# Feed-forward block borders of a fused attention and two-FFN kernel: earlier split of x, and low parts on GpSimd

## The chip, the cores and the metric

One core of one Trainium2 chip runs the whole program. The metric is the device time in microseconds of one execution; several executions were timed, and one more was profiled.

## The reference, cut to what matters

```python
x = attention(q_l, k_l, v_l, q_g, k_g, v_g)          # 4 batches x 544 tokens, 512 features (windowed + global)
xn = x / sqrt(mean(x * x) + 1e-6) * rms_g            # first FFN
g, val = xn @ w_gate, xn @ w_val                     # 512 -> 1536
y = (g * sigmoid(g) * val) @ w_out                   # 1536 -> 512
h = y @ w_in                                         # second FFN, 512 -> 2048
out = (P(h) / Q(h)) @ w_out2                         # a rational function, 2048 -> 512
```

The weights arrive as 64-bit floats and are turned into pairs of 32-bit parts on the chip.

## The kernel before, in words

Three stages follow each other: attention (with part of the first FFN between its steps), the rest of the first FFN, the second FFN. TensorE multiplies float32 data in a reduced form, so every operand is split into a high part (rounded by ScalarE) and a low part (the difference), and each product is three matmuls: high times high, weight low times high, weight high times low.

**First FFN** (class FFN1). The 2176 tokens are cut into 8 blocks (blk) of 288 or 256 tokens, the 1536 hidden features into 3 groups (grp) of 4 tiles k. A *task* is one group of one block; there are 24, all blocks of group 0 first. The generator `units` (L646) gives a task as 12 units:
- `up` (L599): for one k, the products of xt (the split x, four chunks c) with w_gate and w_val into two PSUM banks psg and psv. Two units, chunks 0 and 1, then 2 and 3; 12 matmuls each, at L606 (high x), L607 (weight low) and L608 (low x), chunk by chunk.
- `act` (L610): ScalarE reads psg (L617, or L619 in group 0), VectorE multiplies with psv (L621, and L620 in group 0), ScalarE makes ah (L622), and the low part al (L624) is made by VectorE, or by GpSimd in group 0.
- `down` (L628): 12 matmuls (L633 to L635) of the *previous* task's ah and al with w_out into psA, one of four m a unit; then y is written or added (L639, L641). In a task the four come as one behind the first k and three behind the second.
- `split` (L585): ScalarE writes the high part of the four xt chunks (L595), VectorE the low part (L596), GpSimd in group 0. It is called once a task, behind the last `up`, for the next task. Each xt chunk has one buffer, so its split waits until the last matmul that reads the old chunk is done.

A task is 144 matmuls. **Weights** (class Weights): a conversion takes one tile of 512 columns through ScalarE (L83, L85), VectorE (L91, L92, L95), GpSimd (L99), ScalarE for the high part (L104) and `lo_eng` for the low part (L105). Two scratch tiles cv go round. `step` runs the stages of up to two conversions; in the loop at L884 it is called once a unit from n = 72 on, with VectorE as `lo_eng` (L904). In attention and in the second FFN `lo_eng` is GpSimd.

The order on each engine is not the order of the code: a scheduler places the instructions by priority (the order of the code, unless `high_priority` moves a block ahead by some places) and by its own estimate of durations. Every engine then runs its list strictly in that order, and waits where a row's inputs or buffers are not there. In attention the list `target` (L843 to L846) says how many units are to be placed by each step.

## Time and profile before

| | |
|---|---|
| median of 3 runs | 1089.58 us (1089.46 to 1092.65) |
| profiled execution | 1092.84 us, span 1091.1 us |
| TensorE (PE) busy | 1007.9 us, 92% |
| weight loads (PEld) busy | 907.3 us, 83% |
| VectorE (DVE) busy | 792.8 us, 73% |
| ScalarE (ACT) busy | 600.2 us, 55% |
| GpSimd (POOL) busy | 373.4 us, 34% |

Busy is the share of the span in which an engine has an instruction under way, including time in which that instruction itself is held up. The sum over the span hides the stages: attention ends at about 321 us, the first FFN at about 692 us. The x behind a number counts instructions; in the first FFN the number of matmuls in a stretch says better than the busy share how fast TensorE went.

### The profile page before, as it was taken

The numbers are of one execution on the slowest core, as the hardware profiler recorded it, in microseconds if no ns is written. First come the engines' busy times: TensorE is split into PE (matmuls) and PEld (weight loads), VectorE is DVE, ScalarE is ACT, GpSimd is POOL, SyncE is SP. The second block draws the span as 40 slices with busy tenths as digits, with TensorE's granted clock in tenths as the row PEclk, the third lists the DMA queues.
The fourth block names the chain that finished last, engine by engine and source line by source line (L and its number), as shares of the span: only waits on it lengthen the run. The fifth ranks groups of instructions, "written<-read, shape, count | busy, mean of one in ns | idle before, by whom it ended". The sixth has DMA issues, their size and how long they took to land.

```text
span 1091.1 us, 23781 instructions
## 1 busy us (share of the span) xinstructions
PE 1007.9 (92%) x9368; PEld 907.3 (83%) x9368; DVE 792.8 (73%) x1750; ACT 600.2 (55%) x1347; POOL 373.4 (34%) x421
## 2 busy tenths in 40 slices
PE   3669898998989989999999999999999999999997
PEld 2547777877778889899989999888989989898895
DVE  4674554655529999873797453599898998989987
ACT  3644545645447675552654342466666666666675
POOL 5461212212135743220231111354343543435433
PEclk7669999999999999999999999999999999999999
DMA  7943544434116330650430113500000000000000
GB/s 161 276 127 84 114 123 98 108 100 105 32 39 253 117 116 20 212 174 2 155 117 8 33 40 87 185 1 1 30 1 20 11 1 30 1 30 1 1 31 20
DMA packets 104432, 83.46 MB, mean 76 GB/s; under 512 B 63744, under 2 KB 91392, under 8 KB 104320
## 3 DMA queue, kind: packets, MB, share of 16 engines
q1 hardware_dynamic: 102592, 75.64, 23.8%
q0 software_dynamic: 1728, 6.29, 1.8%
q8 instruction: 74, 1.21, 0.5%
q14 instruction: 38, 0.31, 0.1%
HBM read 62.64 MB, written 10.75 MB: 67 GB/s over the span
## 4 chain that ended last, share of the span: by engine, by line
PE 50%; DVE 29%; ACT 8%; DMA 4%; issue 4%; POOL 3%; SPq 2%; ACTq 0%; POOLq 0%; DVEq 0%
PE psg L606 3%; PE psg L608 3%; DVE q L725 3%; PE psS L349 3%; PE psv L608 3%; DVE q L713 3%; PE psv L607 3%; PE psH L703 3%; PE psH L704 3%; PE psv L606 3%; PE psg L607 3%; PE psH L705 3%; PE psB L738 3%; PE psA L633 3%; PE psB L739 3%
## 5 line engine op out<-in xcount | busy, mean ns | idle before, releaser
L130 POOL TENSOR_SCALAR gh<-p 128x384 fp32r<-128x384 f32 (+1 forms) x96 | 58.1, 605 | 210.2 <-DVE p L727 185.8
L703 PE MATMUL psH<-yt,w_h 128*128 128x384 f32 (+1 forms) x384 | 126.0, 329 | 0.9 <-ACT yt L685 0.7
L704 PE MATMUL psH<-yt,w_h 128*128 128x384 f32 (+1 forms) x384 | 125.4, 327 | 0.0
L705 PE MATMUL psH<-yt,w_h 128*128 128x384 f32 (+1 forms) x384 | 123.5, 328 | 0.9 <-DVE yt L686 0.9
L606 PE MATMUL psg<-xt,w_g 128*128 128x288 f32 (+1 forms) x384 | 114.8, 300 | 7.9 <-ACT xt L595 7.9
L633 PE MATMUL psA<-ah,w_o 128*128 128x288 f32 (+1 forms) x384 | 114.3, 299 | 7.6 <-ACT ah L622 3.8
L608 PE MATMUL psg<-xt,w_g 128*128 128x288 f32 (+1 forms) x384 | 114.2, 299 | 5.3 <-DVE xt L596 4.4
L606 PE MATMUL psv<-xt,w_v 128*128 128x288 f32 (+1 forms) x384 | 112.7, 294 | 1.2 <-DVE a L620 1.1
L738 PE MATMUL psB<-w_p,gh 128*128 128x512 f32 x272 | 108.4, 398 | 5.5 <-POOL gh L130 5.4
L607 PE MATMUL psv<-xt,w_v 128*128 128x288 f32 (+1 forms) x384 | 112.0, 292 | 0.0
L635 PE MATMUL psA<-al,w_o 128*128 128x288 f32 (+1 forms) x384 | 111.5, 291 | 0.5 <-DVE al L624 0.4
L608 PE MATMUL psv<-xt,w_v 128*128 128x288 f32 (+1 forms) x384 | 111.8, 292 | 0.0
L634 PE MATMUL psA<-ah,w_o 128*128 128x288 f32 (+1 forms) x384 | 111.6, 291 | 0.0
L607 PE MATMUL psg<-xt,w_g 128*128 128x288 f32 (+1 forms) x384 | 111.5, 291 | 0.0
L729 POOL TENSOR_TENSOR gl<-p,gh 128x384 fp32r<-128x384 f32 (+1 forms) x96 | 108.6, 1131 | 8.0
L739 PE MATMUL psB<-w_p,gh 128*128 128x512 f32 x272 | 107.2, 394 | 0.0
L723 ACT ACTIVATE r<-q,cq 128x384 f32<-128x384 f32 (+1 forms) x96 | 57.4, 598 | 63.4 <-DVE q L713 62.4
L713 DVE SCALAR_TENSOR_TENSOR q<-q,bv,t 128x384 f32<-128x384 f32 (+1 forms) x96 | 68.8, 717 | 21.7 <-ACT q L711 21.6
L621 DVE SCALAR_TENSOR_TENSOR a<-a,psv 128x256 f32<-128x256 f32 (+1 forms) x96 | 41.6, 434 | 56.5 <-ACT a L617 48.2
L606 PEld LDWEIGHTS psg<-xt,w_g 128*128 128x128 f32 x384 | 73.3, 191 | 10.7 <-ACT xt L595 8.9
L633 PEld LDWEIGHTS psA<-ah,w_o 128*128 128x128 f32 x384 | 73.3, 191 | 10.5 <-ACT ah L622 4.5
L740 PE MATMUL psB<-w_p,gl 128*128 128x512 f32 x272 | 82.1, 395 | 0.0
(173 smaller groups left out, 2815.5 us busy)
## 6 DMA issues: line engine op xcount, KB each, us to landing
vw<-vw SPq DMA_DIRECT2D x64, 130.0 KB, 2.5
raw_h<-in_moe_w_in_dram SPq DMA_DIRECT2D x16, 512.0 KB, 3.8
raw_p<-in_moe_w_out_dram SPq DMA_DIRECT2D x16, 512.0 KB, 4.6
raw_g<-in_moe_w_gate_dram SPq DMA_DIRECT2D x12, 512.0 KB, 4.6
raw_v<-in_moe_w_val_dram SPq DMA_DIRECT2D x12, 512.0 KB, 5.9
raw_o<-in_moe_w_out_dram SPq DMA_DIRECT2D x12, 512.0 KB, 6.8
vw<-in_v_l_dram SPq DMA_DIRECT2D x62, 80.0 KB, 2.5
out_dram<-o SPq DMA_DIRECT2D x17, 256.0 KB, 2.0
```

Source lines behind the costliest of these rows:

```text
L606: nc.tensor.matmul(ps, wh, xt[c][:, 0], start=(c == 0), stop=False)
L607: nc.tensor.matmul(ps, wl, xt[c][:, 0], start=False, stop=False)
L608: nc.tensor.matmul(ps, wh, xt[c][:, 1], start=False, stop=(c == 3))
L633: nc.tensor.matmul(ps, wh, ah, start=(i == 0), stop=False)
L634: nc.tensor.matmul(ps, wl, ah, start=False, stop=False)
L635: nc.tensor.matmul(ps, wh, al, start=False, stop=(i == 3))
L703: nc.tensor.matmul(ph[:, :n], wh, yt[:, c, 0, :n], start=(c == 0), stop=False)
L704: nc.tensor.matmul(ph[:, :n], wl, yt[:, c, 0, :n], start=False, stop=False)
L705: nc.tensor.matmul(ph[:, :n], wh, yt[:, c, 1, :n], start=False, stop=(c == 3))
L729: nc.gpsimd.tensor_tensor(out=gl[:, :n], in0=p, in1=gh[:, :n].bitcast(F32), op=ALU.subtract)
L738: nc.tensor.matmul(acc[m], gh[:, sl], wh, start=(k == 0), stop=False)
L739: nc.tensor.matmul(acc[m], gh[:, sl], wl, start=False, stop=False)
```

## The change

Five edits. (1) `split` works on two chunks at a time: chunks 0 and 1 of the next task are split behind the `up` of chunks 0 and 1 of the last k, chunks 2 and 3 behind the other, both at a priority 60 places ahead. (2) `up` issues the high-x matmuls of both its chunks first (L607 and L608 of the changed kernel), then those with low x (L611). (3) All four `down` units stand behind the second k. (4) GpSimd, no longer VectorE, makes the low parts of xt chunks 2 and 3 in groups 1 and 2, and of every weight converted in the first FFN's own loop. (5) In attention the early target is 6 units, not 7.

```diff
--- before.py
+++ after.py
@@ -527,6 +527,7 @@
     LN2H = 0.34657359027997264
 
     def __init__(self, tc, pool, x, y, gam, wts):
+        self.tc = tc
         self.nc, self.pool, self.x, self.y, self.gam, self.wts = tc.nc, pool, x, y, gam, wts
         nc = self.nc
         self.ones = pool.tile([128, 128], F32, name="ones")
@@ -582,30 +583,32 @@
             v = self.xs(blk, c)
             nc.vector.scalar_tensor_tensor(out=v, in0=v, scalar=self.gam[:, c : c + 1], in1=r, op0=ALU.mult, op1=ALU.mult)
 
-    def split(self, grp, blk):
+    def split(self, grp, blk, cs, xt):
+
         nc = self.nc
         if grp == 0:
             for _ in self.norms[blk]:
                 pass
-        lo = nc.gpsimd if grp == 0 else nc.vector
         nb = self.width(blk)
-        xt = [self.pool.tile([128, 2, NB1], F32R, tag=f"xt{c}", name=f"xt{grp}_{blk}_{c}", bufs=1)[:, :, :nb] for c in range(4)]
-        for c in range(4):
+        for c in cs:
+            lo = nc.gpsimd if grp == 0 or c > 1 else nc.vector
+            xt[c] = t = self.pool.tile([128, 2, NB1], F32R, tag=f"xt{c}", name=f"xt{grp}_{blk}_{c}", bufs=1)[:, :, :nb]
             v = self.xs(blk, c)
-            nc.scalar.activation(out=xt[c][:, 0], in_=v, func=AF.Copy)
-            lo.tensor_tensor(out=xt[c][:, 1], in0=v, in1=xt[c][:, 0].bitcast(F32), op=ALU.subtract)
-        return xt
+            nc.scalar.activation(out=t[:, 0], in_=v, func=AF.Copy)
+            lo.tensor_tensor(out=t[:, 1], in0=v, in1=t[:, 0].bitcast(F32), op=ALU.subtract)
 
     def up(self, k, blk, xt, cs, pss):
         nc = self.nc
+        w = [self.wts.get((j, k)) for j in "gv"]
+        part = lambda j, i, c: w[j][:, i, c * 128 : c * 128 + 128]
+        ps = [p[:, : self.width(blk)] for p in pss]
         for c in cs:
             for j in range(2):
-                w = self.wts.get(("gv"[j], k))
-                wh, wl = (w[:, i, c * 128 : c * 128 + 128] for i in range(2))
-                ps = pss[j][:, : self.width(blk)]
-                nc.tensor.matmul(ps, wh, xt[c][:, 0], start=(c == 0), stop=False)
-                nc.tensor.matmul(ps, wl, xt[c][:, 0], start=False, stop=False)
-                nc.tensor.matmul(ps, wh, xt[c][:, 1], start=False, stop=(c == 3))
+                nc.tensor.matmul(ps[j], part(j, 0, c), xt[c][:, 0], start=(c == 0), stop=False)
+                nc.tensor.matmul(ps[j], part(j, 1, c), xt[c][:, 0], start=False, stop=False)
+        for c in cs:
+            for j in range(2):
+                nc.tensor.matmul(ps[j], part(j, 0, c), xt[c][:, 1], start=False, stop=(c == 3))
 
     def act(self, k, blk, pss, use_silu):
         nc = self.nc
@@ -645,23 +648,25 @@
         prev, xt = None, None
         for i, (grp, blk, use_silu) in enumerate(tasks):
             if xt is None:
-                xt = self.split(grp, blk)
-            acts = []
+                xt = {}
+                self.split(grp, blk, range(4), xt)
+            acts, then = [], {}
             for kk in range(4):
                 k = 4 * grp + kk
                 pss = [self.bank(self.gv, f"ps{j}_{blk}_{k}") for j in "gv"]
-                self.up(k, blk, xt, (0, 1), pss)
-                yield
-                self.up(k, blk, xt, (2, 3), pss)
-                if kk == 3:
-                    xt = self.split(*tasks[i + 1][:2]) if i + 1 < len(tasks) else None
-                acts.append(self.act(k, blk, pss, use_silu()))
-                yield
-                for m in ((0,), (1, 2, 3), (), ())[kk]:
-                    if prev:
+                for cs in ((0, 1), (2, 3)):
+                    self.up(k, blk, xt, cs, pss)
+                    if kk == 3 and i + 1 < len(tasks):
+                        with self.tc.high_priority(offset=60):
+                            self.split(*tasks[i + 1][:2], cs, then)
+                    if cs[0] == 2:
+                        acts.append(self.act(k, blk, pss, use_silu()))
+                    yield
+                if kk == 1 and prev:
+                    for m in range(4):
                         self.down(*prev, m)
                         yield
-            prev = (grp, blk, acts)
+            prev, xt = (grp, blk, acts), then
         for m in range(4):
             self.down(*prev, m)
             yield
@@ -841,9 +846,9 @@
     ffn.set_psum(pp, ("big", banks[0]), ("o", banks[2]))
     for t in range(LAST + 1):
         if t >= SECOND:
-            target[0] = 7 + (IN_ATTN - 7) * (t + 1 - SECOND) / (LAST + 1 - SECOND)
+            target[0] = 6 + (IN_ATTN - 6) * (t + 1 - SECOND) / (LAST + 1 - SECOND)
         elif t >= START:
-            target[0] = 7 * (t + 1 - START) / (SECOND - START)
+            target[0] = 6 * (t + 1 - START) / (SECOND - START)
         with tc.high_priority(offset=50) if t >= START else nullcontext():
             att.step(t, between)
         while done[0] < target[0] - 1:
@@ -901,7 +906,7 @@
             load_2(6 + (blk - 2 * NB) // 2 - 1)
         unit()
         if n >= 72:
-            wts.step(nc.vector, 2 if blk < NB + 1 else 1)
+            wts.step(nc.gpsimd, 2 if blk < NB + 1 else 1)
     for u in range(4):
         unit()
     ps_scope.close()
```

What the scheduler makes of it, at two places. The lines of the changed kernel are numbered a little differently: L597 and L598 are the split (L595, L596 before), L607, L608 and L611 the up products (L606 to L608), L636 to L638 the down products (L633 to L635). A name such as xt1_3_0 is group 1, block 3, chunk 0; ah0_6 is block 0, tile k = 6; psA1_0_0 is group 1, block 0, m = 0. The number behind it is the buffer's.

**TensorE at the border from the task of block 0 to that of block 3 in group 1.** Before:

```order
L633 MATMUL psA1_0_0_6249<-ah0_5_6057,w_o_5_5660 128x288
L634 MATMUL psA1_0_0_6249<-ah0_5_6057,w_o_5_5660 128x288
L635 MATMUL psA1_0_0_6249<-al0_5_6058,w_o_5_5660 128x288
L633 MATMUL psA1_0_1_6306<-ah0_4_5974,w_o_4_5639 128x288
L606 MATMUL psg_3_4_6209<-xt1_3_0_6187,w_g_4_5355 128x256
L607 MATMUL psg_3_4_6209<-xt1_3_0_6187,w_g_4_5355 128x256
L606 MATMUL psv_3_4_6210<-xt1_3_0_6187,w_v_4_5376 128x256
L607 MATMUL psv_3_4_6210<-xt1_3_0_6187,w_v_4_5376 128x256
L606 MATMUL psg_3_5_6266<-xt1_3_0_6187,w_g_5_5423 128x256
L608 MATMUL psg_3_4_6209<-xt1_3_0_6187,w_g_4_5355 128x256
L608 MATMUL psv_3_4_6210<-xt1_3_0_6187,w_v_4_5376 128x256
L633 MATMUL psA1_0_0_6249<-ah0_6_6148,w_o_6_5707 128x288
```

Now:

```order
L637 MATMUL psA1_0_1_6307<-ah0_5_6008,w_o_5_5660 128x288
L636 MATMUL psA1_0_0_6287<-ah0_6_6149,w_o_6_5713 128x288
L637 MATMUL psA1_0_0_6287<-ah0_6_6149,w_o_6_5713 128x288
L638 MATMUL psA1_0_1_6307<-al0_5_6009,w_o_5_5660 128x288
L607 MATMUL psg_3_4_6210<-xt1_3_0_6170,w_g_4_5355 128x256
L608 MATMUL psg_3_4_6210<-xt1_3_0_6170,w_g_4_5355 128x256
L607 MATMUL psv_3_4_6211<-xt1_3_0_6170,w_v_4_5376 128x256
L608 MATMUL psv_3_4_6211<-xt1_3_0_6170,w_v_4_5376 128x256
L607 MATMUL psg_3_4_6210<-xt1_3_1_6173,w_g_4_5355 128x256
L608 MATMUL psg_3_4_6210<-xt1_3_1_6173,w_g_4_5355 128x256
L607 MATMUL psv_3_4_6211<-xt1_3_1_6173,w_v_4_5376 128x256
L608 MATMUL psv_3_4_6211<-xt1_3_1_6173,w_v_4_5376 128x256
```

Before, the low part of chunk 0 (the first L608 rows) is asked for four or five products behind the first use of that chunk. Now the eight products with high x stand together, and the first with low x (L611) come behind them. Ahead of these rows both orders hold down products of the task that has just ended: 7 before and 14 now between the last up product and the first of block 3.

**GpSimd around the same border** (the conversions of w_out tiles 8 to 11 and w_in tile 10). Before:

```order
L99 TENSOR_TENSOR cv32_6543<-cv32_6543,raw_o_8_6024 128x512
L99 TENSOR_TENSOR cv33_6595<-cv33_6595,raw_o_9_6026 128x512
L99 TENSOR_TENSOR cv34_6652<-cv34_6652,raw_o_10_6028 128x512
L99 TENSOR_TENSOR cv35_6726<-cv35_6726,raw_o_11_6030 128x512
L99 TENSOR_TENSOR cv36_6785<-cv36_6785,raw_h_10_6729 128x512
```

Now:

```order
L99 TENSOR_TENSOR cv31_6487<-cv31_6487,raw_v_11_6028 128x512
L105 TENSOR_TENSOR w_v_11_6541<-cv31_6487,w_v_11_6541 128x512
L99 TENSOR_TENSOR cv32_6544<-cv32_6544,raw_o_8_6030 128x512
L105 TENSOR_TENSOR w_o_8_6593<-cv32_6544,w_o_8_6593 128x512
L598 TENSOR_TENSOR xt1_3_2_6194<-x1_1_73,xt1_3_2_6194 128x256
L598 TENSOR_TENSOR xt1_3_3_6197<-x1_1_73,xt1_3_3_6197 128x256
L99 TENSOR_TENSOR cv33_6596<-cv33_6596,raw_o_9_6032 128x512
L99 TENSOR_TENSOR cv34_6659<-cv34_6659,raw_o_10_6034 128x512
L105 TENSOR_TENSOR w_o_9_6656<-cv33_6596,w_o_9_6656 128x512
L105 TENSOR_TENSOR w_o_10_6724<-cv34_6659,w_o_10_6724 128x512
```

Where the list held one add (L99) after the other, each conversion now has two rows (L99 and L105), and the two low parts of x stand between them, behind whatever the rows ahead of them wait for.

On VectorE the 54 rows L105 of the first FFN's loop and 32 of 64 rows L596 are gone. In attention, 24 up or down products stand ahead of the scores of step 6 where 48 stood, 48 instead of 72 ahead of step 8, and 96 in both ahead of step 11; 600 ahead of step 30 in both. From the first row of the second FFN on, the orders of TensorE, VectorE and ScalarE are the same.

## Rows read from the trace of the kernel before

**Rows 1.** Busy time by stage: from:to, length, PE, PEld, DVE, ACT, POOL (instructions), clock.
```profile
321.00:341.00 20.00, 16.28 (x113) 15.58 (x114) 14.34 (x26) 12.95 (x28) 6.77 (x8) 0.91 0.90 322
341.00:485.00 144.00, 134.31 (x1007) 128.96 (x1007) 129.21 (x224) 89.28 (x191) 67.58 (x52) 0.99 0.37 128
520.00:598.00 78.00, 74.09 (x576) 72.55 (x575) 62.98 (x120) 41.72 (x90) 20.10 (x14) 1.00 0.28 95
598.00:692.00 94.00, 94.00 (x746) 94.00 (x745) 42.53 (x98) 32.91 (x75) 11.51 (x14) 1.00 0.24 73
692.00:1092.00 400.00, 387.64 (x1997) 345.05 (x1995) 357.99 (x614) 255.08 (x529) 173.95 (x200) 1.00 0.05 19
```
**Rows 2.** Waits of PE from 341 to 598 us: us in total, times, longest.
```profile
PE psg L608 <- DVE xt L596: 4.4, 8, 0.7
PE psA L633 <- ACT ah L622: 3.8, 3, 2.3
PE psg L606 <- ACT xt L595: 1.7, 3, 0.7
```
**Rows 3.** Timeline of PE and DVE at a border: start, us.
```profile
425.98 1.86 DVE L596 TENSOR_TENSOR xt<-x,xt 128x256 fp32r<-128x256 f32 x2
...
427.89 0.39 PE L608 MATMUL psg<-xt,w_g 128*128 128x256 f32 x1 [0.64 <-DVE xt L596]
```
**Rows 4.** Timeline of POOL at that border.
```profile
426.19 1.36 POOL L99 TENSOR_TENSOR cv<-cv,raw_o 128x512 int32<-128x512 int32 x1 [2.66 <-ACT cv L83]
```
**Rows 5.** DVE lines from 320 to 690 us: ns min/median/max, first and last start.
```profile
L91 DVE TENSOR_SCALAR cv<-cv x54: 411/428/1562, 327.4 to 641.6; 128x512 f32<-128x512 f32 x54
L92 DVE TENSOR_SCALAR cv<-cv x54: 411/427/1425, 327.8 to 643.1; 128x512 int32<-128x512 int32 x54
L95 DVE SCALAR_TENSOR_TENSOR cv<-raw_o,cv x8: 682/692/1303, 364.2 to 425.4; 128x512 int32<-128x512 int32 x8
L105 DVE TENSOR_TENSOR w_v<-cv,w_v x8: 676/685/1477, 338.1 to 414.2; 128x512 fp32r<-128x512 f32 x8
L596 DVE TENSOR_TENSOR xt<-x,xt x64: 409/446/1532, 383.0 to 671.4; 128x256 fp32r<-128x256 f32 x32, 128x288 fp32r<-128x288 f32 x32
L621 DVE SCALAR_TENSOR_TENSOR a<-a,psv x74: 406/442/456, 340.0 to 689.5; 128x288 f32<-128x288 f32 x38, 128x256 f32<-128x256 f32 x36
```
**Rows 6.** POOL lines: L99 from 341 to 485 us, L105 from 0 to 321 us.
```profile
L99 POOL TENSOR_TENSOR cv<-cv,raw_p x6: 1288/1308/1538, 434.9 to 483.1; 128x512 int32<-128x512 int32 x6
...
L105 POOL TENSOR_TENSOR w_v<-cv,w_v x4: 1262/1271/1284, 25.8 to 56.9; 128x512 fp32r<-128x512 f32 x4
```
**Rows 7.** Groups of POOL from 0 to 321 us: count, busy us, mean ns, idle before.
```profile
L624 POOL TENSOR_TENSOR al<-a,ah 128x256 fp32r<-128x256 f32 x12 | 8.9, 741 | 59.9 <-ACT ah L622 41.4 <-PE psA L635 18.5
L624 POOL TENSOR_TENSOR al<-a,ah 128x288 fp32r<-128x288 f32 x9 | 7.4, 822 | 45.1 <-ACT ah L622 26.9 <-PE psA L635 18.2
```
**Rows 8.** Conversions (tile cv) by stretch: length, DVE, ACT, POOL (instructions).
```profile
341.00:485.00 144.00, 89.98 (x131) 42.59 (x66) 49.42 (x34) 0.99 0.37 128
341.00:380.00 39.00, 30.53 (x37) 12.10 (x19) 15.43 (x10) 1.00 0.30 102
520.00:598.00 78.00, 37.71 (x56) 17.91 (x28) 20.10 (x14) 1.00 0.28 95
```
**Rows 9.** Low parts: L596 in two stretches, then L624: length, DVE, POOL.
```profile
341.00:485.00 144.00, 10.73 (x21) 6.52 (x7) 0.99 0.37 128
520.00:598.00 78.00, 9.34 (x16) 0.00 (x0) 1.00 0.28 95
...
341.00:485.00 144.00, 14.98 (x18) 12.16 (x11) 0.99 0.37 128
```
**Rows 10.** All engines from 341 to 380 us, columns as in the first group.
```profile
341.00:380.00 39.00, 36.25 (x272) 34.33 (x272) 35.32 (x51) 26.73 (x59) 30.14 (x25) 1.00 0.30 102
```
**Rows 11.** Waits of PE from 76 to 321 us.
```profile
PE psg L606 <- ACT xt L595: 6.2, 2, 5.1
```
**Rows 12.** ScalarE's high parts of x from 320 to 690 us, columns as in rows 5.
```profile
L595 ACT ACTIVATE xt<-x x72: 400/423/447, 339.4 to 670.9; 128x256 fp32r<-128x256 f32 x36, 128x288 fp32r<-128x288 f32 x36
```

## Prediction

> **What bounds the kernel now.** I read the page first: TensorE is busy 1007.9 of 1091.1 us, so it is the bound over the whole, but that share says nothing about the edited places. So I cut the span by stage [rows 1]. From 598 to 692 us, still first FFN, TensorE does 746 matmuls in 94.00 us without a gap: 0.126 us each. That is its pace when nobody keeps it waiting. From 341 to 485 us (seven tasks) it does 1007, which at that pace are 126.9 us, so 17.1 us are lost; from 520 to 598 us it does 576, which are 72.6 us, so 5.4 us are lost. These 22.5 us are all that the edits can win in the first FFN. The 400 us from 692 us on are the second FFN, whose orders the change leaves alone: no term there.
>
> What sets the two lossy stretches apart is that weights are converted in them: VectorE is busy 129.21 of 144 us and 62.98 of 78, against 42.53 of 94 in the clean one [rows 1]. Next I asked what TensorE waits for there. The waits for the split of x (4.4 us for low parts from VectorE, 1.7 us for high parts) lead, then ah with 3.8 us [rows 2]. These are only the idle times the profile shows; the pace says 22.5 us, since a late matmul's modelled end hides part of a wait. One border shows the mechanism [rows 3, 4]: two low parts take VectorE 1.86 us instead of twice 0.41, because an add on GpSimd runs from 426.19 to 427.55 us; TensorE's first product with a low part starts at 427.89 us, after 0.64 us of idle time.
>
> The lines of VectorE say the same in general [rows 5]. L91, L92, L95, L105 and L596, which read and write SBUF only, have short minima and medians but maxima 0.6 to 1.2 us above them, about one GpSimd instruction. L621, which reads PSUM, stays within 406 to 456 ns. So GpSimd and these VectorE instructions hold each other up, and the sum of their undisturbed times is a load on one shared resource. I call that sum **the pair's load**.
>
> **The pair's load before.** Undisturbed, a conversion costs VectorE 0.411 + 0.411 + 0.682 + 0.676 = 2.18 us, a low part of x or a 0.446 us [rows 5]; on GpSimd the add L99 costs 1.29 us and L105 1.27 us [rows 6], a low part of 256 or 288 columns 0.741 or 0.822, say 0.78 us [rows 7]. From 341 to 485 us, 131 VectorE instructions on cv are 32.75 conversions, 71.4 us; 21 + 18 low parts on VectorE 17.4; 34 adds 43.9; 7 + 11 low parts on GpSimd 14.0 [rows 8, 9]. Together 146.7 us in 144 us: 1.02 a microsecond, a full resource. The heaviest part, 341 to 380 us, carries 9.25 conversions (20.2 us), 10 adds (12.9) and 25 - 10 = 15 low parts on GpSimd (11.7) [rows 8, 10], that is 44.8 us in 39, 1.15 a microsecond: the most that I see it carry for that long. From 520 to 598 us it is 30.5 + 14.3 + 18.1 = 62.9 us in 78, with as many low parts of a as of x [rows 8, 9].
>
> **The change part by part.**
>
> *Low parts to GpSimd.* VectorE loses 33 times 0.676 us and half of 21 times 0.446 in the first stretch, 27 us of its 129. GpSimd gains 33 times 1.27 and 10.5 times 0.78, 50 us on its 67.58 [rows 1]. The pair's load grows by 33 x 0.594 + 10.5 x 0.334 = 23.1 us, to 169.8. The new order moves three conversions out of this stretch (two ahead of it, one behind): 3 x (2.18 - 0.68 + 1.29 + 1.27) = 12.2 us less, 157.6 us. Two bounds for what these take: at the 1.02 that the stretch carried, 154.5 us, 10.5 us **more** than now; if TensorE's own pace is the only bound, 126.9 us, 17.1 less. I take 1.15, since both queues would now be filled the way they were from 341 to 380 us, when GpSimd was busy 30.14 and VectorE 35.32 of 39 us [rows 10]: 137.0 us, **7.0 us less**. In the second stretch the load grows by 14 x 0.594 + 8 x 0.334 = 11.0, to 73.9 us; at TensorE's pace of 72.6 us that is 1.02, under 1.15. So most of its 5.4 us could go, but the 14 conversions stand close together; between 0 and 5.4 I take **2.7 us less**.
>
> *Split earlier, high parts first.* These work on the same 22.5 us and are not added again. They are why I do not go to the upper bound. TensorE now has eight products of about 0.126 us between the first use of a chunk and the first low part, 1 us instead of some 0.5, and 14 instead of 7 down products before that, 0.9 us more. A low part that comes 0.64 us late [rows 3] is covered; one that stands behind two GpSimd instructions of 1.27 us is not. As many matmuls and weight loads as before: no cost.
>
> *Down products later.* Their inputs al are then older; the cover lost is one unit between the first and second k, twelve matmuls of 1.5 us. The scheduler still places them as fillers at the borders, so I price this at nothing, and at most at the 3.8 us of ah waits again [rows 2].
>
> *The moved conversions.* Two more ahead of 341 us are 8.1 us of load. From 321 to 341 us GpSimd is busy 6.77 of 20 us [rows 1], so I price them at nothing; if VectorE's part stands in the way, 8.1 / 1.15 = 7 us.
>
> *What waits behind what.* On GpSimd the low parts of chunks 2 and 3 now stand behind L105, which waits for ScalarE's L104, and the next L83 on ScalarE waits for cv, which L105 frees. With L105 taking 1.27 instead of 0.68 us, ScalarE's ah behind that L83 comes later by up to 0.6 us a conversion. This is inside the 1.02 to 1.15 range.
>
> *Attention.* The split of the very first task, with its wait of 5.1 us, stays where it was; what other waits for x there are come to 1.1 us [rows 11], the most to gain. Against it, five borders with four ScalarE copies of up to 0.43 us (median 0.423) [rows 12] now go ahead of attention's own work: 8.6 us at most. The lower early target moves 24 matmuls, 3 us, either way. I take nothing for all of it.
>
> **Sum.** 7.0 + 2.7 = 9.7 us less. The profiled execution, 1092.84 us, becomes 1083.1; it ran 3.3 us above the median of the runs shown, so the median of 1089.58 becomes **1080** us.
>
> **The rivals.**
>
> *The pair is the bound (slower).* The load does not get cheaper by moving: each low part costs 0.68 us on VectorE and 1.27 on GpSimd. If the pair carries 1.02 as it did over the whole stretch, seven tasks take 154.5 us, and with no gain after 520 us the kernel takes 1089.6 + 10.5 = 1100 us. It decides below 157.6 / 144 = 1.09 a microsecond. For it: VectorE was 90% busy at 1.02 already, mostly by being held up. Against it: the 1.15, and TensorE lost only 39 - 272 x 0.126 = 4.7 of 39 us then [rows 10].
>
> The Trainium skill, SBUF — State Buffer, section "Who interferes with whom", states that a VectorE instruction with two SBUF inputs, or in a two-port mode, and a GpSimd instruction exclude each other for the whole instruction. By that rule the pair could carry 1.00 at most, the stretch would take 157.6 us and the kernel some 1103. That border's 1.86 us agree with the rule, the 1.15 over 39 us says that not the whole of each duration is exclusive.
>
> *Nothing comes of it.* The waits for x go, and those for ah and al, behind longer queues on GpSimd and ScalarE, take their place, or the splits ahead of attention's work give back 8.6 us: 1080 + 8.6, about 1089 us.
>
> *All of it goes.* If the earlier split covers whatever the queues add, TensorE runs at its own pace through both stretches: 1089.6 - 22.5 = 1067 us. Against it speaks a load of 157.6 us in 126.9, 1.24 a microsecond, more than any stretch shows.
>
> **How the numbers follow.** My forecast (1070 to 1086) gets 0.51, all of it 0.11, nothing 0.18, the pair as the bound 0.20. About 0.3%, 3.3 us, is what a measurement of this kernel can tell from no change: faster (under 1086.3) 0.62, the same 0.18, slower (over 1092.8) 0.20. The range reaches from 1067, all of it, to 1097, into the slower case; beyond its ends lie some 0.05 and 0.13.
>
> **What would show it right or wrong.** Right: seven tasks in about 137 us, TensorE's waits for L598 (the low part of x) near zero, VectorE clearly under 90% busy there, GpSimd about 110 us busy or more. The rival: VectorE's L91 and L92 with means above 0.7 us, and new waits of TensorE for ah or for xt from GpSimd. The forecast is wrong altogether if attention ends later than 321 us by more than 4 us, or if the second FFN's 400 us change.

## The result: 1.4% slower, and the profile after

The changed kernel took 1105.43 us (median of four runs, 1104.38 to 1106.88), the kernel before 1089.62 us beside it: ratio 1.0139, 95% interval 1.0118 to 1.0161. The forecast was 1080 us with a range up to 1097; the time lies beyond the range, on the side of the rival "the pair is the bound" (1100 us).

The profiled execution took 1106.88 us with a span of 1105.1, 14.0 us more than before. The stretches of [rows 1] after the change, with the same columns:

```profile
321.00:341.00 20.00, 16.91 (x130) 14.86 (x131) 12.73 (x20) 13.36 (x28) 9.03 (x8) 0.74 0.81 289
341.00:485.00 144.00, 127.26 (x960) 121.78 (x959) 109.47 (x164) 79.75 (x175) 103.90 (x88) 1.00 0.29 99
520.00:598.00 78.00, 74.17 (x577) 72.59 (x576) 51.26 (x92) 39.34 (x84) 38.20 (x31) 1.00 0.28 95
```

From 341 to 485 us VectorE falls from 129.21 to 109.47 us, as meant, and GpSimd rises from 67.58 to 103.90. But TensorE does 960 matmuls where it did 1007. A VectorE that is busy for 76% of the stretch instead of 90% did not make TensorE faster.

The waits of TensorE from 341 to 598 us (us in total, times, longest), the same stretch as in [rows 2], and under them a line of the kernel before that [rows 2] do not show:

```profile
PE psg L611 <- DVE xt L598: 6.1, 10, 1.3
PE psA L636 <- DVE y L644: 4.7, 6, 1.5
PE psA L636 <- ACT ah L625: 4.4, 4, 2.4
PE psg L607 <- ACT xt L597: 4.1, 5, 1.6
PE psv L607 <- DVE a L623: 2.1, 2, 1.1
```
```profile
PE psA L633 <- DVE y L641: 0.5, 1, 0.5
```

The wait for low parts of x from VectorE has grown, 6.1 us where it was 4.4, though VectorE now makes half as many of these low parts. A new wait stands beside it: down products wait 4.7 us for y, where before there was one such wait, of 0.5 us.

VectorE's lines from 320 to 690 us, in the view of [rows 5] (ns min/median/max):

```profile
L91 DVE TENSOR_SCALAR cv<-cv x54: 412/690/1575, 329.2 to 654.3; 128x512 f32<-128x512 f32 x54
L598 DVE TENSOR_TENSOR xt<-x,xt x32: 414/454/1586, 387.4 to 682.8; 128x256 fp32r<-128x256 f32 x16, 128x288 fp32r<-128x288 f32 x16
L624 DVE SCALAR_TENSOR_TENSOR a<-a,psv x72: 406/432/458, 320.1 to 688.8; 128x288 f32<-128x288 f32 x36, 128x256 f32<-128x256 f32 x36
```

The median of L91 rose from 428 to 690 ns with the same minimum; L624, the former L621, which reads PSUM, did not change. So instructions of VectorE that work in SBUF alone are held up more often, in step with GpSimd's extra work. One place shows how that reaches TensorE (timeline, start and us):

```profile
422.12 1.35 POOL L99 TENSOR_TENSOR cv<-cv,raw_g 128x512 int32<-128x512 int32 x1 [1.85 <-issue]
422.23 1.54 DVE L627 TENSOR_TENSOR al<-a,ah 128x288 fp32r<-128x288 f32 x1
...
423.70 0.41 DVE L644 TENSOR_TENSOR y<-y,psA 128x256 f32<-128x256 f32 x1
...
424.17 0.38 PE L636 MATMUL psA<-ah,w_o 128*128 128x256 f32 x1 [1.55 <-DVE y L644]
```

The low part L627 takes 1.54 us instead of 0.45 beside an L99 of GpSimd. The add L644, which empties a bank of psA, stands behind it, and the down product that wants this bank waits 1.55 us.

**Where the 14.0 us lie.** I read the start of every task off its first up product, and the start of the second FFN off its first product into psH. Against before the changed execution is 5.1 us later when the task of block 7 in group 0 starts (345.4 instead of 340.3 us; 1.4 of that before the first up product, and 2.8 between attention's end and this task, where TensorE's granted clock was 0.74 from 321 to 341 us instead of 0.91). The eight tasks from there take 170.1 instead of 162.9 us; three tasks of group 2 take 60.6 instead of 60.1; the second FFN 395.3 instead of 394.1. That is 5.1 + 7.2 + 0.5 + 1.2 = 14.0. "The seven tasks" below are the first seven of these eight: 148.8 instead of 144.6 us.

Single profiles have scatter. Four kernels with the same order in attention as before differ by 3.6 us from the first up product to the last product of attention, and seven with the changed order there by 5.1 us. Much of it goes with TensorE's clock, which the trace shows at two levels, 1.0 and 0.5 (2.4 and 1.2 GHz): two of the four ran 14.6 us of attention at 0.5 and took 245.0 and 245.1 us, the other two 6.7 and 6.8 us and took 241.5 and 241.6. Hence the verdicts below go by the ratios of many executions, and the profiles only say in which stage a difference lies.

### The profile page after: what moved, and what is told of

Read it like the earlier page. It is cut to its first block, busy times and chain, and to the rows that moved or that the text cites. A ratio compares the mean times of both kernels' runs of the same rounds, so it can differ in the third digit from the quotient of the medians.

```text
span 1105.1 us, 23815 instructions
## 1 busy us (share of the span) xinstructions
PE 1003.7 (91%) x9368; PEld 904.2 (82%) x9368; DVE 770.9 (70%) x1664; ACT 597.9 (54%) x1347; POOL 465.3 (42%) x508
## 4 chain that ended last, share of the span: by engine, by line
PE 46%; DVE 25%; ACT 8%; POOL 6%; issue 6%; DMA 5%; SPq 3%; ACTq 0%; POOLq 0%; DVEq 0%
PE psg L607 3%; DVE q L718 3%; DVE q L730 3%; PE psH L708 3%; PE psH L709 3%; PE psH L710 3%; PE psB L743 3%; DVE cv L91 3%; PE psB L744 3%; PE psB L745 2%; PE psS L349 2%; PE psg L611 2%; PE psv L607 2%; PE psv L611 2%; PE psv L608 2%
## 5 line engine op out<-in xcount | busy, mean ns | idle before, releaser
L636 PE MATMUL psA<-ah,w_o 128*128 128x288 f32 (+1 forms) x384 | 114.5, 301 | 11.7 <-DVE y L644 6.0
L607 PE MATMUL psg<-xt,w_g 128*128 128x288 f32 (+1 forms) x384 | 112.8, 299 | 9.6 <-ACT xt L597 9.6
L607 PE MATMUL psv<-xt,w_v 128*128 128x288 f32 (+1 forms) x384 | 111.0, 293 | 2.3 <-DVE a L623 2.1
L611 PE MATMUL psg<-xt,w_g 128*128 128x288 f32 (+1 forms) x384 | 104.7, 296 | 6.7 <-DVE xt L598 6.1
L638 PE MATMUL psA<-al,w_o 128*128 128x288 f32 (+1 forms) x384 | 109.8, 292 | 0.1
L608 PE MATMUL psg<-xt,w_g 128*128 128x288 f32 (+1 forms) x384 | 109.8, 290 | 0.0
L608 PE MATMUL psv<-xt,w_v 128*128 128x288 f32 (+1 forms) x384 | 109.7, 289 | 0.0
L611 PE MATMUL psv<-xt,w_v 128*128 128x288 f32 (+1 forms) x384 | 103.0, 291 | 0.0
L598 POOL TENSOR_TENSOR xt<-x,xt 128x256 fp32r<-128x256 f32 (+1 forms) x64 | 53.8, 859 | 93.8 <-ACT xt L597 93.7
L636 PEld LDWEIGHTS psA<-ah,w_o 128*128 128x128 f32 x384 | 73.7, 193 | 16.5 <-DVE y L644 7.7
L91 DVE TENSOR_SCALAR cv<-cv 128x512 f32<-128x512 f32 x68 | 49.5, 727 | 51.1 <-ACT cv L83 50.9
L624 DVE SCALAR_TENSOR_TENSOR a<-a,psv 128x256 f32<-128x256 f32 (+1 forms) x96 | 41.4, 433 | 62.1 <-ACT a L620 53.3
```

The lines of the kernel that those rows point to most:

```text
L607: nc.tensor.matmul(ps[j], part(j, 0, c), xt[c][:, 0], start=(c == 0), stop=False)
L608: nc.tensor.matmul(ps[j], part(j, 1, c), xt[c][:, 0], start=False, stop=False)
L611: nc.tensor.matmul(ps[j], part(j, 0, c), xt[c][:, 1], start=False, stop=(c == 3))
L636: nc.tensor.matmul(ps, wh, ah, start=(i == 0), stop=False)
L638: nc.tensor.matmul(ps, wh, al, start=False, stop=(i == 3))
```

## Experiments

All ratios are to the kernel before, run beside it on the same chip; the brackets hold the 95% interval.

### Which part costs

**w_low_back, x_low_back, both_back**: the changed kernel with low parts back on VectorE, those of the weights, those of x, or both (then only the order edits are left).

```diff
-            wts.step(nc.gpsimd, 2 if blk < NB + 1 else 1)
+            wts.step(nc.vector, 2 if blk < NB + 1 else 1)
```
```diff
-            lo = nc.gpsimd if grp == 0 or c > 1 else nc.vector
+            lo = nc.gpsimd if grp == 0 else nc.vector
```

> The changed kernel with one edit undone: the weights' low parts (L105) in the first FFN's loop go back to VectorE. Pair theory (GpSimd and VectorE's SBUF instructions hold each other up, and the low parts cost 1.27 us there instead of 0.68): the pair's load falls by 19.6 us in the seven converting tasks, at the 1.06 a microsecond of the changed kernel some 18 us, so about 1088 us, and the eight tasks that took 170.1 us take about 155 to 160. Order theory (later down products or the splits ahead of other work cost the time, not the engine): stays at 1103 or more, eight tasks near 170 us.

> The changed kernel with the low parts of x chunks 2 and 3 back on VectorE in groups 1 and 2. Pair theory: 0.33 us less load for each of some 11 low parts in the stretch, 4 us, so 1101 to 1103 us. Queue theory (the low parts of x stand on GpSimd behind L105 and come late for TensorE): the waits of TensorE for x go and the kernel gains 5 us or more, 1100 us or less. Order theory: 1105 us.

> The changed kernel with both low parts back on VectorE: only the order edits are left (split by chunks and ahead, high parts first, all down products behind the second up, target 6). Pair theory: the engine edits were the loss, the order edits gain some part of the 6 us of waits for x, so 1083 to 1089 us. Order theory: 1100 us or more.

Measured: 1100.68 us, 1.0077 [1.0056, 1.0099]; 1099.12 us, 1.0069 [1.0047, 1.0092]; 1098.78 us, 1.0059 [1.0038, 1.0080]. By the ratios either move of low parts gives back 0.6 to 0.7%, and both together 0.8%, of the 1.39% that were lost. So the engine edits are somewhat more than half of the loss. The other 0.59%, 6.4 us, remains with the order edits alone, which I had priced at nothing.

The pair theory had expected more in two of the three runs (1088 us, and 1083 to 1089 us): it took the whole loss for its own. x_low_back is in the range of the queue theory, but the wait that this theory wanted gone grew from 6.1 to 9.2 us (L611 for VectorE's low parts, 340 to 615 us), so its time does not speak for it.

**only_w_low, only_down**: the kernel before with one edit alone, the weights' low parts on GpSimd (the first diff above, turned round), or all four down products behind the second k (the diff below).

```diff
-                for m in ((0,), (1, 2, 3), (), ())[kk]:
+                for m in ((), (0, 1, 2, 3), (), ())[kk]:
```

> The kernel before with one edit made: the weights' low parts in the first FFN's loop on GpSimd. Pair theory: the load grows by 19.6 us in the seven converting tasks and by 8.3 us in the second stretch, where some room is left; 1100 to 1108 us, the seven tasks 10 us or more longer than their 144. Order theory: within 4 us of 1089.6.

> The kernel before with one edit: all four down products behind the second up. Bank theory: psA has three banks (two in attention), four down products in a row need the first bank again, which comes free when VectorE has added it to y, behind its conversions; so waits of TensorE for y (L641) rise from 0.5 us to 2 us or more between 341 and 598 us and the kernel is 2 to 6 us slower, 1092 to 1096. Rival (down products are only fillers, the place in the code hardly matters): 1088 to 1092 us.

Measured: only_w_low 1101.35 us, 1.0077 [1.0053, 1.0100]; only_down 1094.12 us, 1.0022 [1.0007, 1.0037]. The 54 moved low parts of weights cost 0.8%, some 8 us, by themselves, with every other edit left out. In the profile the seven tasks take 149.2 instead of 144.6 us, a smaller step than the 10 us or more expected, and the three tasks of group 2, where other conversions stand, 64.5 instead of 60.1.

**no_down, only_target, no_high_first**: all order edits but the down products' place; the early target of 6 alone; all order edits but high parts first. Low parts as before in all three.

> The order edits without the down products' new place: split by chunks and ahead, high parts first, target 6, low parts as before. Bank theory: the y waits go and the kernel loses 2 to 6 us against the 1098.8 of all order edits, 1093 to 1096. Splits theory (the splits ahead of other work or the high parts first are the loss): stays at 1097 or more.

> The kernel before with one edit: 6 units, not 7, in the early target of attention. If the later units cost time, attention ends later and the kernel takes 1092 us or more, up to the 3 us that all order edits show up to the start of the sixth task. If that was scatter, 1088 to 1092 us.

> All order edits except the high parts first: the products of a chunk stand together again, low part third. If high first helps as forecast (1 us more until the first low part), this is slower than the 1098.8 us of all order edits, 1100 to 1104, with longer waits of TensorE for low parts. If it costs (both banks stay open longer, the last products stand later in the order), 1092 to 1097.

Measured: no_down 1089.22 us, 0.9979 [0.9961, 0.9997]; only_target 1091.83 us, 1.0010 [0.9994, 1.0025]; no_high_first 1093.71 us, 1.0021 [1.0005, 1.0036]. Without the down products' move the order edits are slightly faster than before, faster than either theory had them. The move costs 0.2% alone and some 0.8% together with high parts first (1.0059 against 0.9979): an interaction, which the last group of runs takes up.

### The pair's load by itself

**w_low_on_act** takes work off VectorE without giving it to GpSimd. ScalarE writes a scaled copy in place of the weight's low part: the low part's value is left out, its place, size and readers stay.

```diff
+        if lo_eng is nc.vector:
+            nc.scalar.activation(out=out[:, 1], in_=vf, func=AF.Copy, scale=2.0**-13)
+        else:
+            lo_eng.tensor_tensor(out=out[:, 1], in0=vf, in1=out[:, 0].bitcast(F32), op=ALU.subtract)
```

**pool_extra** does the reverse: GpSimd gets work and VectorE keeps all of its own. In group 1 it adds each ah into a scratch tile that nobody reads.

```diff
+        if 4 <= k < 8:
+            ...
+            nc.gpsimd.tensor_tensor(out=self.spin[:, :nb], in0=self.spin[:, :nb], in1=ah.bitcast(F32), op=ALU.add)
```

> The kernel before, where in the first FFN's own loop ScalarE writes the weight's low part as a scaled copy of the same tile: this leaves out the value of that low part, and keeps its place in the chain, its size and who reads it. VectorE loses 54 instructions of 0.68 us (36 us), GpSimd gains none, ScalarE gains 54 of some 0.63 us. Theory 'pair's load': the load of the seven tasks falls from 146.7 to some 124 us, below TensorE's own 127 us; the eight tasks from 163 to 150 to 156 us, the kernel to 1079 to 1085 us. Theory 'the chain of the conversions and the in-order queues, not the shared port': ScalarE now has the work ahead of ah instead, 1089 us or more.

> The kernel before, and beside it GpSimd adds ah into a scratch tile that nobody reads, once for each k of group 1: 32 adds of some 0.78 us, 25 us, about the load that the change adds to the pair in the seven tasks; all of VectorE's work stays where it was. Theory 'pair's load': VectorE's L91, L92 and L596 get longer by about what is added, while L621, which reads PSUM, does not, and the eight tasks take 10 to 25 us more: 1099 to 1114 us. Theory 'GpSimd has room, and only a moved instruction's place in a queue counts': within 4 us of before.

Measured: w_low_on_act 1078.65 us, 0.9891 [0.9872, 0.9911]; pool_extra 1104.27 us, 1.0124 [1.0101, 1.0147]. The first is just under its range, the second inside it. Below are the seven tasks of w_low_on_act and of pool_extra (columns of [rows 1]); then pool_extra's rows of the added work and of an L621 that shares the stretch with it; then L596 from 320 to 690 us, first before and then in pool_extra (busy us and mean ns behind the bar):

```profile
338.70:473.30 134.60, 128.26 (x1011) 126.68 (x1011) 103.14 (x189) 103.18 (x223) 60.28 (x51) 1.00 0.39 134
```
```profile
344.10:497.50 153.40, 138.94 (x1012) 133.73 (x1011) 139.32 (x225) 89.37 (x193) 84.46 (x71) 0.96 0.36 121
```
```profile
L629 POOL TENSOR_TENSOR spin<-spin,ah x32: 733/938/1248, 398.5 to 559.3; 128x256 f32<-128x256 f32 x16, 128x288 f32<-128x288 f32 x16
...
L621 DVE SCALAR_TENSOR_TENSOR a<-a,psv x71: 405/422/456, 321.9 to 686.7; 128x256 f32<-128x256 f32 x36, 128x288 f32<-128x288 f32 x35
```
```profile
L596 DVE TENSOR_TENSOR xt<-x,xt 128x256 fp32r<-128x256 f32 (+1 forms) x64 | 32.0, 511 | 3.0 <-ACT xt L595 2.7
```
```profile
L596 DVE TENSOR_TENSOR xt<-x,xt 128x256 fp32r<-128x256 f32 (+1 forms) x64 | 39.0, 621 | 2.2 <-ACT xt L595 1.9
```

With the low parts on ScalarE (103.18 us busy, 89.28 before) the seven tasks need 134.6 us, 10 less. With some 14 us more of useless GpSimd work in them (18 adds of 0.78 us) they need 153.4, 9 more. A GpSimd add of 733 ns at least has a median of 938: it is held up too.

Two other causes could stand behind pool_extra. One is the in-order queue: each add waits for ah ahead of the next L99. The trace speaks against it: from the end of L95, which makes the input of L99, to the start of L99 the 34 conversions of these tasks lose 9.7 us in all, as many as in the kernel before. What did get longer is VectorE's own work: its instructions without PSUM, 170 (171 before), sum to 129.4 us instead of 119.5, while the 54 with PSUM take 23.1 and 23.2. The other is TensorE's clock, at 0.5 for 13.7 us of these tasks instead of 3.4. In attention 7.9 us more at 0.5 went with 3.5 us more time (before against only_w_low); at that price the 10.3 us here are worth some 4.6 of the 9 us, an estimate. The low clock came during or right behind waits of 1.4 to 2.4 us, so some of the price of a late input is paid through the clock.

**after_no_down**: the changed kernel, down products as before. **no_down_relief**: no_down, and group 0's low parts that fall behind attention go from GpSimd to VectorE.

```diff
-            lo = nc.gpsimd if grp == 0 else nc.vector
+            lo = nc.gpsimd if grp == 0 and blk < 6 else nc.vector
...
-        lo = nc.vector if use_silu else nc.gpsimd
+        lo = nc.vector if use_silu or k > 3 or blk > 5 else nc.gpsimd
```

> The changed kernel with the down products put back (one behind the first k, three behind the second); low parts on GpSimd, the earlier split, high parts first and target 6 stay. The order edits without the down products gave 1089.2 us on the old engines, the GpSimd edits alone some 8 us of their own (weights) and 5 to 6 us when taken out of the changed kernel. Theory 'two causes that add': 1089 + 6 to 9 = 1095 to 1099 us. Theory 'the down products' place is the main cause, and the GpSimd edits hurt mainly through it': 1092 us or less, and TensorE's waits for y in the changed kernel (5.3 us) go. Theory 'the pair's load alone': 1099 to 1101 us, the eight tasks from the last of group 0 on still 167 us or more.

> The order edits without the down products (1089.2 us, ratio 0.9979), and the low parts of group 0 that fall behind attention (blocks 6 and 7, and the first tiles of group 1) moved from GpSimd to VectorE: some 7 low parts of x and 11 of a, each 0.33 us cheaper on VectorE, 6 us less load of the pair in the seven tasks. Theory 'pair's load': the stretch from the first of these tasks on gets 4 to 6 us shorter, 1083 to 1086 us. Theory 'VectorE's own queue is the bound': VectorE gets 8 us more work, 1089 us or more.

Measured: after_no_down 1097.55 us, 1.0062 [1.0041, 1.0083], 0.8% over no_down, which is again what the engine edits cost. no_down_relief 1089.77 us, 0.9988 [0.9969, 1.0006]: no gain, and in the range of its rival, that VectorE's own queue is the bound. Its load fell by 8 us and the seven tasks by 1.4.

The table counts the instructions between the first up product of the first of the seven tasks and that of the task behind them, at the undisturbed prices of [rows 5 to 7]. The last column is the time in them with TensorE's clock at 0.5:

| kernel | load, us | seven tasks, us | load per us | clock at 0.5, us |
|---|---|---|---|---|
| w_low_on_act | 121.4 | 134.6 | 0.90 | 0.0 |
| no_down_relief | 135.5 | 140.2 | 0.97 | 3.4 |
| no_down | 143.3 | 141.6 | 1.01 | 3.4 |
| both_back | 146.7 | 148.8 | 0.99 | 3.4 |
| before | 147.2 | 144.6 | 1.02 | 3.4 |
| no_high_first | 147.6 | 151.1 | 0.98 | 17.1 |
| after_no_down | 153.5 | 144.8 | 1.06 | 3.4 |
| changed kernel | 154.9 | 148.8 | 1.04 | 0.0 |
| only_w_low | 156.1 | 149.2 | 1.05 | 10.2 |
| after_silu_hf_late | 158.3 | 146.6 | 1.08 | 3.4 |
| pool_extra | 160.8 | 153.4 | 1.05 | 13.7 |

No kernel carries more than 1.08 over these tasks, however the rest is ordered. In the changed kernel an instruction of GpSimd, or one of VectorE without PSUM, is under way for 93% of these tasks, before for 90%, in w_low_on_act for 82%: with the heavier loads the pair is nearly full. At 140 us of load and below, the load no longer seems to set the time alone: VectorE's own list, which no_down_relief lengthened, and TensorE's 127 us may count as well.

Load is not all of it, though. Kernels of like load differ by 4.2 us (both_back against before), and by 6.5 us where the clock was low for long (no_high_first). The order edits alone, with the load of before, make the seven tasks as long as in the changed kernel, 148.8 us. What the engine edits add there is seen in what is left undone: both_back places 33 of the L99 in them, the changed kernel 29, and its next task takes 21.3 us where both_back's takes 18.4.

### What the order edits cost

**both_back_acc4** is both_back with a fourth PSUM bank for the down products, taken from the up products.

```diff
-    ffn.set_psum(pp, ("gv", 5), ("acc", 3))
+    ffn.set_psum(pp, ("gv", 4), ("acc", 4))
```

> Only the order edits (low parts on the engines of before), but with four PSUM banks for the down products and four for the up products, instead of three and five. With three and five it ran in 1098.8 us against 1090.6 before. Theory 'the fourth down product of a task waits for a bank that VectorE has not yet added to y': TensorE's waits for y (2.2 us) vanish and the time falls to 1089 to 1094 us. Theory 'it is not the banks, but the order alone': 1097 us or more. A fourth bank for the downs is taken from the ups, which may cost a few microseconds of its own: a time over 1100 us would leave this open.

Measured: 1097.69 us, 1.0075 [1.0049, 1.0101], against 1.0059 with three. The waits for y are gone from TensorE's list, and nothing is gained; ah (5.4 us) and the high part of x (5.2 us) lead it now. Waits for a bank were a symptom, or the up products missed theirs as much: the run can't say which, but a bank is not the cure.

**The switch to silu.** The profiles of the four kernels with moved down products and the low parts of before show a wait of TensorE of 2.0 to 2.8 us for the high part of x at the start of one task of group 1. ScalarE's timeline in both_back, and the product that waits:

```profile
405.11 0.63 ACT L104 ACTIVATE w_v<-cv 128x512 fp32r<-128x512 f32 x1 [1.36 <-POOL cv L99]
405.65 0.68 ACT L85 ACTIVATE raw_o<-raw_o 128x512 int32<-128x512 uint32 x1
406.34 1.28 ACT L620 ACT_TABLE_LOAD   x1
407.63 0.38 ACT L620 ACTIVATE a<-psg 128x256 f32<-128x256 f32 x1
407.91 0.65 ACT L83 ACTIVATE cv<-raw_v 128x512 f32<-128x512 f32 x1
408.47 0.62 ACT L104 ACTIVATE w_g<-cv 128x512 fp32r<-128x512 f32 x1
408.99 0.43 ACT L597 ACTIVATE xt<-x 128x288 fp32r<-128x288 f32 x1
```
```profile
409.47 0.61 PE L607 MATMUL psg<-xt,w_g 128*128 128x288 f32 x1 [2.72 <-ACT xt L597]
```

The program changes from tanh to silu when 96 units are placed. With the down products moved, unit 96 falls behind the act of the second k instead of on it. One more k takes the tanh form, and ScalarE's table load of 1.28 us moves from the middle of a task (393.76 us in the kernel before, where TensorE waits for nothing from 392 to 398 us) to the border, ahead of the split. Three runs put the switch one unit earlier, which is the k of before:

```diff
-        if n == 12 * NB:
+        if n == 12 * NB - 1:
```

> Only the order edits, with the switch to silu one unit earlier, so that the same k as before is the first with silu. Theory 'the late switch puts the table load ahead of a split': the 2.7 us wait of TensorE for the high part of x at the border to the task of block 0 in group 1 goes, the eight tasks take 163 to 165 us instead of 167.2, the kernel 1094 to 1097 us instead of 1098.8. Theory 'the down products' own place costs it': 1098 us or more. Theory 'the switch is the whole of it': 1089 to 1092 us.

> The kernel before with all four down products behind the second k, and the switch to silu back at the same k as before. With the late switch it ran in 1094.1 us against 1090.9 (ratio 1.0022). Theory 'the late switch': the 2.2 us wait for the high part of x at that border goes, ratio 0.999 to 1.001. Theory 'the down products' own place': ratio 1.002 or more as before.

> The changed kernel with the switch to silu one unit earlier. Theory 'the late switch': the wait of 2.4 us for ah behind the table load goes, 1101 to 1103 us instead of 1105.4, the pair's load still costing its part. Theory 'it makes no difference, since the pair's load sets the pace there anyway': 1104 to 1107 us.

Measured: both_back_silu 1096.67 us, 1.0052 [1.0033, 1.0070] (1.0059 with the late switch); only_down_silu 1090.95 us, 1.0004 [0.9988, 1.0020] (1.0022); after_silu 1103.81 us, 1.0120 [1.0092, 1.0148] (1.0139). Each is lower by 0.1 to 0.2%, but in all three the intervals of early and late switch overlap, so the gain is not shown; all three point the same way, and the down products' move alone is then no longer to be told from before. The wait is not the table load's alone either: at that border it is 1.9 us in both_back_silu instead of 2.7, and no_down, whose table load stands in the middle of a task, has one of 2.1 us at another border. A small term at most, and some 0.5% of the order edits was still open.

**High parts first, behind attention alone.** In the profiles attention, from the first up product to its last own product (with 720 feed-forward products in between in every kernel), takes 242.6 to 248.1 us where the high parts come first, in ten kernels, and 239.9 to 245.1 in eight without. Two runs keep the old order of the up products in attention:

```diff
                 nc.tensor.matmul(ps[j], part(j, 1, c), xt[c][:, 0], start=False, stop=False)
+                if k < 4 and blk < 6:
+                    nc.tensor.matmul(ps[j], part(j, 0, c), xt[c][:, 1], start=False, stop=(c == 3))
+        if k < 4 and blk < 6:
+            return
```

> The changed kernel with the switch to silu put back, and high parts first only in the tasks behind attention (blocks 6 and 7 of group 0, and groups 1 and 2); the ups in attention stand as before. Theory 'high parts first costs in attention, where the up products fill gaps': attention some 3 to 6 us shorter, the kernel 1098 to 1101 us instead of 1103.8, and what is left over 1090.9 is the pair's load (the weights' low parts alone gave 8.4 us). Theory 'attention's spread is only scatter': 1102.5 us or more.

> The version with the early split, target 6 and high parts first, low parts and down products as before (1089.2 us against 1090.9, ratio 0.9979), now with high parts first only behind attention. Theory 'high parts first costs in attention': 1084 to 1087 us, ratio 0.994 to 0.997, faster than both kernels. Theory 'only scatter': ratio 0.997 to 0.999 as before.

Measured: after_silu_hf_late 1096.97 us, 1.0062 [1.0046, 1.0079], against 1.0120 with high parts first everywhere: 0.6% gained. Attention takes 239.5 us in it and 247.3 in after_silu, the rest of the first FFN 386.4 and 386.7: in these two profiles all of it lies in attention. no_down_hf_late 1088.15 us, 0.9982 [0.9970, 0.9995], where no_down had 0.9979: no gain, as the theory "only scatter" had it. So high parts first cost in attention only together with the moved down products. The other profiles agree: with both edits in attention it takes 243.0 to 248.1 us (seven kernels), with the moved down products alone 239.5 to 241.5 (four), with high parts first alone 242.6 to 244.1 (three), with neither 241.1 to 245.1 (six).

What it is in attention shows in two figures of TensorE. Behind the first up product it waits 20.9 to 23.8 us in attention in the seven kernels with both edits, and 15.7 to 18.6 us in the thirteen others. And its clock stands at 0.5 for longer: in after_silu for 22.0 us of attention, in after_silu_hf_late for 12.6. Of the 7.8 us between these two, 5.8 are waits (22.7 against 16.9 us), and 9.4 us more at 0.5 are worth some 4.2 at the price of 3.5 us for 7.9 (an estimate; the two overlap). One place in after_silu shows both, a wait for VectorE's qgz and then the clock (column before the last two) from 262 to 273 us; after_silu_hf_late has neither there:

```profile
265.62 0.93 PE L372 MATMUL psT<-ident,p 128*128 128x128 f32 x4 [1.72 <-DVE qgz L334]
```
```profile
262.00:265.80 3.80, 1.51 (x37) 0.94 (x26) 3.72 (x12) 1.51 (x4) 2.75 (x3) 1.00 0.25 55
265.90:269.20 3.30, 3.30 (x74) 2.91 (x73) 3.23 (x14) 1.24 (x4) 0.00 (x0) 0.50 0.71 163
269.40:273.00 3.60, 3.60 (x30) 3.37 (x29) 0.84 (x2) 1.24 (x4) 0.29 (x1) 1.00 0.28 62
```

Why the order makes these waits is argued, not shown: the up products fill gaps in attention, and the scheduler spreads them otherwise. When 52 of attention's 64 psX products are done, both kernels have 588 feed-forward products behind them, but after_silu needs 208 us from the first up product and after_silu_hf_late 203; at the 60th it is 7 us behind. In the changed kernel no feed-forward product stands between 117.2 and 131.6 us, so attention runs into its own input load. The DMA queue and TensorE's product behind it in the changed kernel, then TensorE's waits between 90 and 140 us in after_silu_hf_late:

```profile
124.45 1.23 SPq L278 DMA_DIRECT2D vw<-vw  x2
125.78 1.16 SPq L233 DMA_DIRECT2D kin<-in_k_l_dram  x2
127.05 0.95 SPq L245 DMA_DIRECT2D qin<-in_q_l_dram  x2
```
```profile
130.00 0.66 PE L309 MATMUL psQ<-ident,qin 128*128 128x128 f32 x2 [5.04 <-DMA qin<-in_q_l_dram]
```
```profile
PE psO L382 <- DMA vw<-vw: 2.2, 1, 2.2
...
PE psQ L309 <- DMA qin<-in_q_l_dram: 1.6, 1, 1.6
```

The kernel before, which has 12 down products and then up products in this stretch, waits nowhere for qin. But after_silu (5.2 us for qin) and after_silu_hf_late (1.6 and 2.2) differ here by 1.4 us only. The rest of the waiting is spread over many waits of at most 1.7 us, most of them for results of attention on VectorE and ScalarE.

**A version that beats both.** no_down and no_down_hf_late are faster than the kernel before by 0.2%, with upper bounds at 0.9997 and 0.9995: above chance, hardly more. w_low_on_act is no version, as it leaves a value out, but shows where 1.1% lie.

## Why the prediction was wrong, point by point

**The step that failed** is the rate: "I take 1.15, since both queues would now be filled the way they were from 341 to 380 us". The load itself was right: 157.6 us forecast, 154.9 counted. But the seven tasks carried it at 1.04 a microsecond, took 148.8 us instead of 137, and left conversions over for the next task (21.3 instead of 18.3 us). I knew the point at which the rival wins, 1.09, and set aside the 1.02 of the whole stretch for the best 39 us in it; over seven tasks every kernel of the table stays between 0.90 and 1.08. I also misread those 39 us. "TensorE lost only 4.7 of 39 us then" is 12%, the same share as the 17.1 of 144 us in the whole stretch: they gave no sign that TensorE waits less when the pair carries more. Forecast -7.0 us, measured +4.2 for the seven tasks and +7.2 with the next one. Of the 23.7 us between the forecast for the profiled execution and its time, these seven tasks make 11.2, and not by the engine edits alone, since both_back takes 148.8 us too.

**The rule of exclusion.** The Trainium skill, SBUF — State Buffer, section "Who interferes with whom", calls the port pair that VectorE and GpSimd share an exclusive lock, which a VectorE instruction in a two-port mode holds for its whole length and for which one with two SBUF inputs contends with a GpSimd instruction that reads SBUF. By that the pair could carry 1.00 a microsecond at most. The kernels carry up to 1.08, so the measurement does not bear it out to the last tenth. The trace does agree on who is affected: L91 and L598 stretch, L624 with its PSUM operand does not. That the 1103 us worked out from it, and the 1100 us of the rival, came near the measured 1105 is luck in part: they had the seven tasks at 157.6 and 154.5 us, not 148.8, and nothing for attention and the switch, which make 0.8% together.

**The second stretch**: -2.7 us forecast, +0.5 measured; the three tasks of group 2 in it had a load of 51.4 us in 60.1 before and of 61.5 us in 60.6 now, again 1.02 a microsecond.

**Order edits and down products at nothing.** "The scheduler still places them as fillers at the borders, so I price this at nothing" held for the move alone once the switch was put back (1.0004). In the whole change it did not: no_down shows that the order edits with the down products cost 0.8% more than without. I priced the place of instructions on TensorE and overlooked what is tied to the count and order of units elsewhere: the switch to silu (some 0.2% if it is real) and the fillers of attention.

**Attention at nothing.** I named up to 8.6 us against it for ScalarE's copies at the borders, and took none of it. High parts first together with the moved down products cost 0.6% there; undoing that alone, with ScalarE's early copies left in, gave it back, so it is not the copies. In its place the profiles show TensorE waiting longer for attention's own inputs and results, and longer at the low clock.

**What would show it**: two of my four signs came true or nearly (VectorE at 76% in the stretch, GpSimd at 103.90 of 110 us) although the forecast was wrong. They only showed that the work had moved. The two that were about TensorE (137 us, no waits for L598) failed. Of the rival's, the means of L91 and L92 rose over 0.7 us from 341 to 485 us (838 and 748 ns, where they were 608 and 633); the waits for ah and for xt from GpSimd hardly changed (4.4 and 0.6 us against 3.8 and 0.6), and the new waits were for y instead.

The chain from before to the changed kernel, by ratio: 1 to 1.0062 with all edits but the late switch, and high parts first behind attention alone; 1.0120 with them in attention too; 1.0139 with the late switch. That the first step is the engine edits is what only_w_low (1.0077) and after_no_down against no_down (0.8%) show. That they cost it as load of the pair, and not by their place in a queue, rests on pool_extra and w_low_on_act; no_down_relief, where VectorE's list grew as the load fell, shows that the load is not the only bound.

## What to carry to other kernels

Moving work from a busy engine to an idle one can lose time where the two hold each other up: price the sum of both engines' durations, and take its rate over the whole stretch, not over its best part. When an edit changes how many steps lie between two places, look for everything that counts them: here a table switch and the fillers of another stage. Let signs of success be about the engine that sets the end, not about the work that was moved.

## What the runs showed of the hardware that was not expected

GpSimd's own instructions are held up in the same way as VectorE's: in pool_extra an add has a minimum of 733 ns and a median of 938. GpSimd was busy for 47% of the seven tasks before, and 14 us more work on it made them 9 us longer. So a busy share of half does not mean room.

A switch of ScalarE's tables takes 1.28 us. In the middle of a task (before) no wait of TensorE stood beside it; ahead of a split TensorE waited 2.0 to 2.8 us, though not for the table load alone.

TensorE's clock takes part in what looks like scatter. In both_back it stood at 0.5 from 409.0 to 412.4 us, at the border where TensorE waited 2.72 us; in no_high_first it did so for 17.1 us of the seven tasks, the slowest of all. Two kernels with the same order in attention differed by 3.5 us with 14.6 and 6.7 us at 0.5 (before and only_w_low). Not every such stretch stands behind a long wait: before has one from 163.0 to 166.4 us with no wait over 0.3 us in the 6 us ahead of it.
